# A second pair of token blocks in seven half-size products, and a weight matrix converted early and kept in DRAM

## The chip, the core and the metric

The kernel runs on one NeuronCore of a Trainium2 chip. Its engines work in parallel and each runs its own instructions in order: TensorE (PE; PEld is its weight load), VectorE (DVE), ScalarE (ACT), GpSimd (POOL) and SyncE (SP), which here issues all DMAs. The metric is the device time of one execution in microseconds (us); the compared figure is the median over runs.

## The reference

Three operators follow one another on 4 batches of 576 tokens and 512 channels (8 heads of 64), all in float32 (some weights arrive as float64).

```python
out_up    = repeat(sm_attn(mean4(q), mean4(k), mean4(v)), 4)      # pooled attention, 144 x 144
out_local = softmax(where(|i-j| < 4, q k^T / 8, -1e9)) @ v        # banded attention
x  = out_up + out_local                                           # (4, 576, 512)
u  = x + (relu(x^T @ w_tok1) @ w_tok2)^T                          # token mixing, 576 -> 256 -> 576
x  = u + relu(u @ w_ch1) @ w_ch2                                  # channel mixing, 512 -> 1536 -> 512
th = x @ w_theta
y  = w_tok_r @ (x * cos(th)) + w_tok_i @ (x * sin(th))            # per batch, 576 x 576 each
u  = x + y
result = u + relu(u @ w_ch)
```

## The kernel before, in words

**Numbers.** A float32 product is three matmuls (`mm3`, lines 142 to 146): high x high, high x low, low x high, where `high` is the value rounded to TensorE's reduced float32 and `low` the remainder. Every weight arrives as 8-byte words and goes through `converted` (line 153) one block of 128 rows at a time: a DMA into `raw`; two ScalarE steps (180, 181); three VectorE steps (183, 185, 193); one GpSimd addition (197); ScalarE's cast to `high` (199); VectorE's subtraction for `low` (201). A `yield` between these lets other work stand between them.

**Stages.** (a) Attention and token mixing, by pairs and quads of heads; the result u goes to DRAM (`uT`). (b) Channel mixing's first pass: hidden columns 0 to 511 (`LOWER` = 2 parts of 256), for six blocks of 384 tokens; the partial sum goes to DRAM (`xT`). It is interleaved with attention. (c) Channel mixing's second pass: hidden columns 512 to 1535, blocks 2 and 3, then 0 and 1, then 4 and 5. A dense block is `mix` with p0 = 2: 8 column blocks of 12 matmuls for the first layer, then 4 output blocks of 24 (lines 654 to 657). Blocks 0 and 1 are a pair: the first layer over both token blocks and halves of the channels is a 2 x 2 block product, done in seven half-size products (`pair_product`, 6 matmuls for each of 4 m). That needs sums of weight blocks (`weight_parts`, 64 steps), sums of token blocks (`pair_sum`) and additions on the way out of PSUM (`pair_hidden`). Output goes to `xT` (columns) and, transposed, to `xN` (rows). (d) The last stage, by batch: theta (lines 1081 to 1121), y (1123) with the row matrix `wr` (w_tok_r and w_tok_i, 9 blocks of 128 x 576), and the output (1183), also in seven products, with sums of `wc`.

**Order.** Stages (a) to (c) run in an order written out by hand: `ORDER` (line 30) is a list of step names, and each mention advances that step's generator to its next `yield`, so the list sets the instruction order on all five engines, SyncE's DMA issues included. Names: P, W, K, L, A: loads and steps of a head pair; V, F, T, E, U: pooled attention, token mixing, u's store; C, H, O: load, hidden and output of a block in the first pass, B, M, N in the second; S: weight sums; PL, PS, PT, PP, PH: load, split, sums, products and hidden of a pair; D: output blocks of a paired block; X: weight conversions (X8 to X23 second pass, X24 to X27 w_theta, X28 to X36 the row matrix, X37 to X40 w_ch); R: memory released and allocated; Z and ZS: batch 0 of stage (d) loaded and split. The last stage's order is set by the framework from the program's order.

In before X28 to X36 stand between D1 and N1.3 and beside B4, X24 to X27 and X37 to X40 beside B5; pools for late weights follow one another (`late_weights`, 935), and `load_x` (967) loads x and its rows xn together.

Of the kernel before, what the change touches and what calls it, by code (L numbers as in the profile page):

```python
# [41 lines left out]
X3 X6 L11*2 C0 L11 P15 U3.1*2 A8 F6 U3.1 C0 F5 T4 L11 L12 L10 O0.1 K15 C0 C1 W11 L10 O0.0 C0 T4*2 F7 O0.3 O0.2 L12 C1  # L42
O0.3 T4 L12 F7 L12 T4 C1 L11 E4.1 F6 L11 F7 L11 F6 C1 A10 W12 E4.0 L11 F6 F7 E4.0 A11 F7 L12 E4.1 C1 H1.0 T5 C2 F6
L13*2 H1.1 L12 H1.1 T4 T5 T4 U4.0 L13 C1 U4.0 H1.0 U4.0 L13 V7 T4 H1.2 T5 L13 L15 L13 T4 U4.1 L12 U4.1 L15 L12 W15 V7
C1 H1.2 A12 V7 U4.1 T5 H1.3 V7 H1.3 L13 E5.0 C1 L13 F7 C1 F7 E5.0 F7 L15 L14*2 A13 L15 C1 O1.0 L14 F7 O1.1 L14 T5 W14
C1 E5.1 C2 E5.1 T6 L14 L15 L14 T5 T6 T5 U5.0 C2 T5 U5.0 L15 U5.0 T5 O1.2 T6 O1.3*2 L15 L14 T6 U5.1 L14 U5.1*2 L15 T6
E6.0 A14 A15 C2 E6.1 C3 E6.0 T7 E6.1 T6 T7 H2.0 T6 U6.0 H2.0 T7*2 U6.0*2 C3 T6*2 T7 U6.1*2 E7.0 U6.1 C2 E7.1*2 E7.0 T7
H2.1*2 T7 U7.0 T7 U7.0*2 T7 C2*2 H2.2 U7.1 H2.2 U7.1 C3 U7.1 R0 X8 X17 H2.3 X11 H2.3 C2 X19 C2*2 X8 O2.1 X8 C2 O2.2 X8
O2.0 X11 C3 O2.3*2 X21 C3 H3.0 X19 H3.0 X19 X8 C3 X17 X8 X17 C4 H3.1 C3 H3.2*2 X17 H3.1 X19 X20 H3.3 X21 H3.3 C3 X11
X9 C3 C4 O3.0 X21 X17 X19 C3 C4 X21 C3 O3.2 X11 X21 X13 C4 O3.3 O3.1 X21 O3.3 X12 X17 X9 C4 X9 X20 X19 C4 X9 H4.0 X13  # L50
H4.0 X20 C5 C4 X15 H4.2 H4.1 X9 H4.1 X20 H4.2 H4.3 B2 X16 H4.3 C4 X9 X13 C4 C5 X13 X20 C4 O4.1 X12 X10 C5 X13 C4 O4.2
X12 B2 C5 O4.0 X12 X11 X13 C5 O4.3 H5.0 X20 X16 O4.3 X23 B2 C5 H5.1 X10 H5.0 X10 C5 H5.2 X12 X11 X10 H5.1 B2 H5.3 X14
X10 H5.3 J2 H5.2 X16 C5 M2.4 X23 X10 X16 X23 X15 C5 X18 C5 O5.1 X23 X22 B2 O5.2 O5.0 X12 X15 X14 C5 X23 X14 X16 M2.5
# [12 lines left out]
N1.0 X30 X31 N1.0*2 B4 D1 N1.1 B4 X28*2 X29 D1 N1.2 X28 X30 X29 X32 X28 X30 X29 X33 X29 N1.3 X30 X28 X29 X31 X34 N1.1
D0 N1.2 N1.1 X30 X31 D0 X32 N1.2 N0.0 X31 X30 X32 X33 X35 D0 X31 N0.1 X32 N0.0 N0.1 N0.0 X31 X32 X33 X34 X36 D0 N0.1
N0.2 X33 X32 N0.2 X35 X34 N0.2 X33 B4 N0.3 X34 X33 B4 N0.3 M4.4 X34 X35 N0.3 X36 B4 N0.3 M4.4 X35 M4.5 X34 M4.5 B4
M4.6 X36 X35 B4 M4.7 M4.6 X36 M4.7 J4 X35 X36 B4 N1.3 M4.8 N1.3 X36 M4.8 B4 M4.9 N1.3 M4.9 B4 M4.10*2 B5 M4.11*2 R6
X24 X25 X26 Z B4*2 N4.0*2 B5 N4.0 B5 X24 B4 X24 X25 N4.1 X26 X24 X25 X27 X24 X26 B4 X25 X37 X25 N4.2 X26 X24 X25 X38  # L70
X26 N4.1 B5 N4.3 N4.1 X26 B5 M5.4*2 N4.2*2 B5 M5.5 X27 M5.5 B5 X27 X37 M5.6 X37 X38 X27 B5 X39 X27 M5.6 X37 M5.7 B5
X27 M5.8 X38 X40 X37 B5 M5.9 X37 X38 M5.7 M5.8 X38 B5 M5.9 X39 X38 N4.3 M5.10 M5.11 M5.10 M5.11 X39 N4.3 X40 N4.3 X39
X40 X39*2 X40 B5 X40*2 B5 J5 R2 ZS*4 B5 ZS N5.0 N5.1 N5.0 N5.1 N5.0 ZS*2 B5 N5.2 N5.1 ZS N5.2*2 N5.3*4

# [3 lines left out]
PAIRS = ((0, 1),)  # L78
LOWER, WIDE = 2, 2
MIX = 384  # L80
# [25 lines left out]
def kernel(  # L106
# [23 lines left out]
    xN_d = dram.tile([B * S, DM], F32, name="xN")  # L130

# [21 lines left out]
    def converted(stage, hi, lo, parts, sub, add, gaps=repeat(1), room=None):  # L153

        n, at, gap = math.prod(hi.shape[1:]), next(serial), iter(gaps)
# [16 lines left out]
        if len(hi.shape) == 3:  # L172
            hi, lo = (t.rearrange("p k n -> p (k n)") for t in (hi, lo))
# [31 lines left out]
        yield  # L205

# [117 lines left out]
    weight, cells = {}, {}  # L324
    lowsteps = []
# [384 lines left out]
    def pair_room(n):  # L710
        two[n]["uh"], two[n]["ul"] = (b1.tile([128, 4, MIX], F32R, tag=f"u{p}", name=f"u{p}_p{n}") for p in "hl")

    def pair_load(n):
        i, j = PAIRS[n]
        t = two[n] = {}
        t["u"] = cells["utx"].tile([128, 4, MIX], F32, tag="ut", name=f"u_p{n}")
# [5 lines left out]
        t["th"], t["tl"] = (  # L722
            [cells["T"].tile([128, 2, MIX], F32R, tag=f"t{p}{k}", name=f"t{p}{k}_p{n}") for k in range(4)] for p in "hl"
        )
        t["last"] = t["tl"][2]
        sp.dma_start(t["last"].bitcast(F32), columns(uT_d, j)[:, 0:2])
        yield

    def pair_split(n):
        t = two[n]  # L730
        pair_room(n)
# [6 lines left out]
    def pair_sum(n, k):  # L738
# [14 lines left out]
    def pair_product(n, m, i):  # L753
# [14 lines left out]
        right = {  # L768
            1: (t["uh"][:, 0:2], t["ul"][:, 0:2]),
            2: (t["uh"][:, 2:4], t["ul"][:, 2:4]),  # L770
            3: (t["qh"], t["ql"]),
        }
        for e, k in ((5, 0), (6, 1), (7, 2), (4, 3)):
            right[e] = t["th"][k], t["tl"][k]
# [578 lines left out]
```

## Time and profile before

| | us |
|---|---|
| median of 3 runs | 685.97 |
| lowest, highest | 682.52, 691.41 |
| the profiled execution | 682.84 |
| its span, first to last instruction | 680.9 |

The profile is of one execution. PE stands for TensorE's matmuls, whose ends are modelled, so a busy PE need not be PE at its peak; DVE is VectorE, ACT ScalarE, POOL GpSimd, SP SyncE. Line numbers (L144) are those of the kernel before; a helper's line covers every use of it, and the names of the operands tell them apart (`wrl<-ww,wrh`: the low part of the row matrix from the working tile and the high part).

### The profile page before, as it was taken

How to read it: one execution, taken by the hardware profiler on the slowest of the kernel's cores; microseconds unless marked ns; L12 is line 12 of the kernel's file. 1: busy time of each engine (PE TensorE's matmuls, PEld its weight loads, DVE VectorE, ACT ScalarE, POOL GpSimd, SP SyncE). 2: the span in 40 equal slices, each digit the busy share in tenths (PEclk: the TensorE clock that was granted, in tenths of full speed). 3: DMA queues.
4: the chain of work that ended last, by engine and by line, in shares of the span. 5: the costliest groups of instructions: out<-in, count | busy, mean ns of one | idle time of the engine just before them, and what ended most of it. 6: DMA issues, size and time to landing. Idle time of an engine off the chain costs nothing.

```text
span 680.9 us, 17322 instructions
## 1 busy us (share of the span) xinstructions
PE 659.3 (97%) x7344; PEld 630.2 (93%) x7344; DVE 508.5 (75%) x916; ACT 317.2 (47%) x618; POOL 91.8 (13%) x79
## 2 busy tenths in 40 slices
PE   7869999999999999999999999999999999999997
PEld 4658879999999999999999999999998998998997
DVE  5879998764543788997656996987887848857837
ACT  4566667353442564533222553544637326526311
POOL 3223332201000432300000231330000000000000
PEclk9879999999999999999999999999999999999999
DMA  8796787554334686217434668954030420140202
GB/s 284 250 282 218 253 273 256 171 183 143 106 129 158 200 280 198 74 38 186 86 101 145 215 126 270 303 147 114 1 132 0 154 72 0 62 141 1 70 1 70
DMA packets 85629, 100.36 MB, mean 147 GB/s; under 512 B 44272, under 2 KB 65904, under 8 KB 85552
## 3 DMA queue, kind: packets, MB, share of 16 engines
q1 hardware_dynamic: 85552, 99.27, 46.5%
q8 instruction: 57, 0.93, 0.6%
q14 instruction: 20, 0.16, 0.1%
HBM read 74.34 MB, written 24.90 MB: 146 GB/s over the span
## 4 chain that ended last, share of the span: by engine, by line
PE 89%; DVE 4%; DMA 4%; ACT 1%; SPq 1%; issue 0%; POOL 0%; DVEq 0%; ACTq 0%; POOLq 0%
PE c L654 6%; PE c L144 6%; PE c L657 6%; PE c L655 6%; PE c L145 6%; PE c L146 6%; PE y L144 6%; PE y L145 6%; PE y L146 6%; PE th L144 2%; PE th L146 2%; PE th L145 2%; PE t L144 2%; PE t L146 2%; PE t L145 2%; PE c_p L849 2%
## 5 line engine op out<-in xcount | busy, mean ns | idle before, releaser
L197 POOL TENSOR_TENSOR ww<-ww,raw 128x512 int32<-128x512 int32 (+2 forms) x43 | 60.4, 1407 | 285.1 <-ACT ww L180 93.6
L144 PE MATMUL y<-wrh,zh 128*128 128x288 f32 x256 | 75.0, 296 | 0.0
L145 PE MATMUL y<-wrl,zh 128*128 128x288 f32 x256 | 74.9, 296 | 0.0
L146 PE MATMUL y<-wrh,zl 128*128 128x288 f32 x256 | 72.8, 295 | 0.0
L144 PEld LDWEIGHTS y<-wrh,zh 128*128 128x128 f32 x256 | 48.0, 188 | 0.0
L145 PEld LDWEIGHTS y<-wrl,zh 128*128 128x128 f32 x256 | 48.0, 188 | 0.0
L146 PEld LDWEIGHTS y<-wrh,zl 128*128 128x128 f32 x256 | 47.2, 188 | 0.0
L180 ACT ACTIVATE ww<-raw 128x512 f32<-128x512 f32 (+2 forms) x43 | 29.2, 679 | 30.7 <-DMA raw<-w_ch 9.8
L144 PE MATMUL c<-uh,c1h 128*128 128x384 f32 x128 | 42.8, 334 | 0.0
L146 PE MATMUL c<-uh,c1l 128*128 128x384 f32 x128 | 42.8, 334 | 0.0
L145 PE MATMUL c<-ul,c1h 128*128 128x384 f32 x128 | 42.8, 334 | 0.0
L865 DVE SCALAR_TENSOR_TENSOR g<-c,g 128x384 fp32r<-128x384 f32 x56 | 29.5, 548 | 16.8 <-ACT g L862 16.8
L862 ACT ACTIVATE g<-c 128x384 fp32r<-128x384 f32 x56 | 26.5, 490 | 28.6 <-PE c L146 28.5
L1133 DVE TENSOR_TENSOR cx<-y,cx 128x288 f32<-128x288 f32 x32 | 14.6, 456 | 32.0 <-PE y L146 31.6
L873 DVE TENSOR_TENSOR ut<-c,ut 128x384 f32<-128x384 f32 x40 | 21.4, 550 | 18.6 <-PE c L657 18.2
L139 ACT CAST cuh<-cx 128x288 fp32r<-128x288 f32 (+1 forms) x16 | 8.8, 553 | 50.3 <-DVE cx L1133 50.3
L181 ACT ACTIVATE raw<-raw 128x512 int32<-128x512 uint32 (+3 forms) x48 | 31.7, 661 | 0.0
L144 PE MATMUL th<-thh,cxh 128*128 128x512 f32 (+1 forms) x92 | 31.6, 343 | 0.0
L145 PE MATMUL th<-thl,cxh 128*128 128x512 f32 (+1 forms) x92 | 31.6, 343 | 0.0
L193 DVE SCALAR_TENSOR_TENSOR ww<-raw,ww 128x512 uint32<-128x512 uint32 (+2 forms) x43 | 30.4, 707 | 1.5
L146 PE MATMUL th<-thh,cxl 128*128 128x512 f32 (+1 forms) x92 | 31.2, 343 | 0.0
L185 DVE TENSOR_SCALAR ww<-ww 128x512 uint32<-128x512 uint32 (+2 forms) x43 | 25.0, 581 | 1.5
(361 smaller groups left out, 2110.4 us busy)
## 6 DMA issues: line engine op xcount, KB each, us to landing
raw<-w_ch SPq DMA_DIRECT2D x28, 512.0 KB
qk<-qkT SPq DMA_DIRECT2D x16, 582.0 KB
xT<-ut SPq DMA_DIRECT2D x12, 768.0 KB
vd<-vtok SPq DMA_DIRECT2D x8, 650.0 KB
raw<-w_ri SPq DMA_DIRECT2D x9, 576.0 KB
vw<-vloc SPq DMA_DIRECT2D x32, 146.2 KB
uT<-us SPq DMA_DIRECT2D x16, 288.0 KB
ut<-uT SPq DMA_DIRECT2D x6, 768.0 KB
```

The costliest lines, as they stand in the source:

```text
L144: pe.matmul(out, lh, rh, start=start, stop=False, skip_group_check=again)
L145: pe.matmul(out, lh, rl, start=False, stop=False, skip_group_check=again)
L146: pe.matmul(out, ll, rh, start=False, stop=stop, skip_group_check=again)
L180: act.activation(w, high, AF.Abs)
L181: act.activation(f, words[:, :, 0], AF.Copy, scale=2.0**-29)
L193: dve.scalar_tensor_tensor(out=wu, in0=words[:, :, 1], scalar=0xC0000000, in1=wu, op0=ALU.bitwise_and, op1=ALU.bitwise_or)
L197: pool.tensor_tensor(out=w.bitcast(I32), in0=w.bitcast(I32), in1=f, op=ALU.add)
L654: pe.matmul(ps[:, 0:MIX], h[:, cb % 2, d], h1, start=cb == cbs[0], stop=False)
L655: pe.matmul(ps[:, 0:MIX], l[:, cb % 2, d], h1, start=False, stop=False)
L657: pe.matmul(ps[:, 0:MIX], weight[cb // 2][2][:, cb % 2, d], h2, start=False, stop=cb == cbs[-1])
L862: act.activation(h1, ps, AF.Relu)
L865: dve.scalar_tensor_tensor(out=h2, in0=ps, scalar=0.0, in1=h1.bitcast(F32), op0=ALU.max, op1=ALU.subtract)
```

## The change

`PAIRS` becomes ((0, 1), (5, 4)): blocks 5 and 4 go through the pair's path instead of the dense one. The tiles of `pair_sum` are joined to one per sum; the second pair's raw u is loaded into the tile of its low part. The row matrix is converted in attention, in eleven steps X28 to X38 (nine of 512 columns, one of 8 x 64, one of 64) whose high and low parts stand in `raw` itself and are stored to DRAM (`wr_d`); they are read back by ten loads (LR) beside D4 and D5. The four blocks of w_theta are converted beside the first pair and D1, into rooms of other tiles; w_ch's first two blocks (X41, X42) likewise, kept in DRAM (`wc_d`) and read back at the end (LC), its other two (X43, X44) beside D4 and D5. Batch 0's x is loaded beside D4, its rows xn at the end of D5, when the buffer `utx` of block 4's output is free. In the last stage the split of the next x is placed after the first additions and casts of y, and the weight sums use another tile.

The order, from the first X28 on, and from D1 on (steps up to X28 stand as before, and between the two excerpts the second pass's blocks 2 and 3 and the first pair are only shuffled, with X24, X25 and X27 begun beside the pair):

```diff
-X3 X6 L11*2 C0 L11 P15 U3.1*2 A8 F6 U3.1 C0 F5 T4 L11 L12 L10 O0.1 K15 C0 C1 W11 L10 O0.0 C0 T4*2 F7 O0.3 O0.2 L12 C1
+X3 X6 X28 X29 X30 L11*2 C0 X28 L11 P15 X29 U3.1*2 A8 X28 F6 U3.1 C0 F5 T4 X29 X28 L11 L12 L10 O0.1 K15 C0 C1 X28 X29
+W11 L10 X28 X29 O0.0 C0 T4 X30 X28 T4 F7 O0.3 O0.2 L12 C1 O0.3 X31 T4 L12 F7 L12 T4 C1 L11 E4.1 F6 L11 X29 F7 L11 F6
...
+PH0.3.2 X41 X25 PL1 PH0.2.4 PL1 PH0.3.4 PL1 PH0.2.4 X25 PH0.3.4 D1*2 PH0.2.4 X25 N1.0 PH0.3.4 X25 N1.0 X27 N1.0 X25
+X27 X41 D1 X26 N1.1 X27 X41 PS1 X27 N1.1 D1 X41 N1.2 N1.1 PT1.0 X41 N1.2 X27 N1.2 X41 X26 N1.3 X41 PT1.0 X26 PT1.0 X26
+D0 N1.3 PT1.1 X26 N1.3 D0 X26 PT1.1 J0 PT1.1 N1.3 PT1.3 PS1 PT1.3 D0 PT1.3 PS1 N0.0 N0.1 N0.0 PT1.2 D0 N0.0 N0.2 PT1.2
+PS1 N0.1 PT1.2 N0.1 PP1.0.1 N0.3 N0.2 PP1.1.1 PH1.0.1 N0.2 PP1.0.3 PH1.1.1 PP1.1.3 N0.3*2 PP1.0.2 PP1.1.2 PH1.0.2 N0.3
...
+PH1.3.4 PH1.2.4 PH1.3.4 PH1.2.4 D4 PH1.3.4 R5 Z D4 N4.0 X43 LR N4.0 LR N4.0 LR D4 N4.1 LR N4.1*2 LR D4 N4.2 LR X43*2
+N4.3 R6 X43 ZS N4.2 ZS N4.2 X43 ZS X43 D5 LR ZS N4.3 LR ZS D5 X44 N5.0 N4.3 ZS N5.0 ZS N4.3 ZS LR*2 D5 N5.1*2 D5 N5.2
+X44 N5.2 X44 R6 Z X44 N5.3*2 LC X44 N5.3 X44 N5.3 LC N5.0 N5.1 N5.2
```

The code, cut to its core:

```diff
-PAIRS = ((0, 1),)
+PAIRS = ((0, 1), (5, 4))
...
+    wr_d = [dram.tile([128, 9, S], F32, name=f"wr_{e}") for e in "hl"]
+    wc_d = [dram.tile([128, 2, DM], F32, name=f"wc_{e}") for e in "hl"]
...
-    def converted(stage, hi, lo, parts, sub, add, gaps=repeat(1), room=None):
+    def converted(stage, hi, lo, parts, sub, add, gaps=repeat(1), room=None, keep=()):
...
+        if keep:
+            hi, lo = (raw.bitcast(F32R)[:, e * n : e * n + n] for e in range(2))
...
+        for dst, t in zip(keep, (hi, lo)):
+            t = t.bitcast(F32)
+            sp.dma_start(dst, t.rearrange("p (k n) -> p k n", k=dst.shape[1]) if len(dst.shape) == 3 else t)
+        if keep:
+            yield
...
+    late = []
+    for k in range(9):
+        r, c = slice(k * 128, k * 128 + 128), slice(0, 512)
+        late.append((w_ri[r, c], [t[:, k, c] for t in wr_d]))
+    c = slice(512, S)
+    late.append((w_ri[0:1024, c].rearrange("(k p) n -> p k n", p=128), [t[:, 0:8, c] for t in wr_d]))
+    late.append((w_ri[1024:1152, c], [t[:, 8, c] for t in wr_d]))
+
+    def early(k):
+        src, keep = late[k]
+        return converted(stg, None, None, [(0, 128, src)], *ENDS, keep=keep)
...
+        rooms = [(b2, "ut")] * 3 + [(cells["T"], f"t{k}") for k in (0, 1)] + [(b2, "ut")]
+        late_weights(24, range(4), rooms, w_theta, into=cells["th"])
+        late_weights(41, range(2), rooms[4:], w_ch, keep=wc_d)
...
+    def load_weights(name, d, groups):
+        for a, b in groups:
+            for t, src in zip(cells[name], d):
+                sp.dma_start(t[:, a:b].bitcast(F32), src[:, a:b])
+                yield
...
     def after_pair():
+        for name, old in (("cs", "hx"), ("cn", "utx")):
+            cells[old].release()
+            cells[name] = ctx.enter_context(tc.tile_pool(name=name, bufs=1, side="right"))
+            yield
...
     def first_load():
-        cells["x0"] = load_x(0)
+        cells["x0"] = [load_x(0)]
+        yield
+        cells["x0"].append(load_rows(0))
         yield
...
+    step("LR", lazily(lambda: load_weights("wr", wr_d, ((8, 9), (0, 2), (4, 6), (2, 4), (6, 8)))))
+    step("LC", lazily(lambda: load_weights("wc", wc_d, ((0, 2),))))
...
-    sb1 = ctx.enter_context(tc.tile_pool(name="c1p", bufs=1))
+    sb1 = ctx.enter_context(tc.tile_pool(name="c1p", reuse_waits="tile", bufs=1))
...
-            xx = load_x(b + 1)
+            x1 = load_x(b + 1)
+            with tc.issue_after(cells["x loads"].ins):
+                xx = x1, load_rows(b + 1)
             xhl, steps = split_x(b + 1, xx[0])
-            for st in steps:
-                st()
+            with tc.issue_after(added.ins), tc.issue_after(cast.ins):
+                for st in steps:
+                    st()
```

## Rows read from the trace of the kernel before

**Rows 1.** The page: busy us, share, instructions; granted clock in 40 slices.

```profile
PE 659.3 (97%) x7344; PEld 630.2 (93%) x7344; DVE 508.5 (75%) x916; ACT 317.2 (47%) x618; POOL 91.8 (13%) x79
...
PEclk9879999999999999999999999999999999999999
```

**Rows 2.** Stretches: us, PE, PEld, DVE, ACT, POOL, PEclk, DMA share, GB/s.

```profile
0.00:104.00 104.00, 86.51 (x2462) 70.50 (x2463) 87.50 (x170) 61.84 (x146) 32.15 (x35) 0.93 0.81 261
60.00:104.00 44.00, 40.65 (x1142) 35.79 (x1142) 41.11 (x79) 29.28 (x69) 13.17 (x11) 1.00 0.80 262
104.00:677.00 573.00, 572.81 (x4884) 559.72 (x4882) 419.90 (x745) 255.31 (x473) 59.61 (x44) 1.00 0.41 127
104.00:128.00 24.00, 24.00 (x471) 21.87 (x471) 21.31 (x39) 15.52 (x38) 8.76 (x8) 1.00 0.65 210
104.00:212.00 108.00, 108.00 (x1947) 102.00 (x1946) 63.59 (x115) 50.45 (x113) 12.05 (x11) 1.00 0.48 155
284.00:332.00 48.00, 48.00 (x277) 47.74 (x276) 42.87 (x89) 18.62 (x37) 1.52 (x1) 1.00 0.39 103
332.00:362.00 30.00, 30.00 (x174) 30.00 (x173) 15.59 (x30) 6.72 (x14) 0.00 (x0) 1.00 0.29 74
402.00:452.00 50.00, 50.00 (x290) 50.00 (x289) 42.20 (x65) 25.22 (x46) 12.45 (x9) 1.00 0.75 225
```

**Rows 3.** Waits of TensorE, whole span: us in total, times, longest.

```profile
PE o L523 <- DVE pbuf L501: 4.0, 1, 4.0
```

**Rows 4.** The chain in order of time: start us, us, what.

```profile
418.94 1.04 PE c L657 x6
423.10 1.04 PE c L657 x6
```

**Rows 5.** Groups of first-layer matmuls: shapes, count, busy us, mean ns.

```profile
L144 PE MATMUL c<-uh,c1h 128*128 128x384 f32 x128 | 42.8, 334 | 0.0
...
L144 PE MATMUL p_a<-uh_p,c1h 128*128 128x384 f32 x16 | 5.4, 335 | 0.0
```

**Rows 6.** Pair and eviction work of VectorE: count, ns min/median/max.

```profile
L748 DVE TENSOR_TENSOR tl_p<-z_p,th_p x4: 946/952/958, 320.3 to 331.6; 128x768 fp32r<-128x768 f32 x4
...
L735 DVE TENSOR_TENSOR ul_p<-u_p,uh_p x1: 1750/1750/1750, 325.3 to 325.3; 128x1536 fp32r<-128x1536 f32 x1
...
L873 DVE TENSOR_TENSOR ut<-c,ut x40: 512/550/560, 132.9 to 466.8; 128x384 f32<-128x384 f32 x40
```

**Rows 7.** Groups of one weight conversion's steps: busy us, mean ns | idle before.

```profile
L185 DVE TENSOR_SCALAR ww<-ww 128x512 uint32<-128x512 uint32 x32 | 17.7, 554 | 1.1
L193 DVE SCALAR_TENSOR_TENSOR ww<-raw,ww 128x512 uint32<-128x512 uint32 x32 | 22.2, 693 | 1.1
L201 DVE TENSOR_TENSOR wrl<-ww,wrh 128x576 fp32r<-128x576 f32 x9 | 13.2, 1474 | 0.0
L201 DVE TENSOR_TENSOR c11l<-ww,c11h 128x512 fp32r<-128x512 f32 x2 | 1.4, 682 | 0.0
L180 ACT ACTIVATE ww<-raw 128x512 f32<-128x512 f32 x32 | 21.6, 676 | 21.9 <-DMA raw<-w_ch 9.8 <-DVE c1l L201 9.5 <-issue 1.6
L199 ACT CAST c1h<-ww 128x512 fp32r<-128x512 f32 x8 | 4.9, 614 | 2.5 <-POOL ww L197 2.5
L197 POOL TENSOR_TENSOR ww<-ww,raw 128x576 int32<-128x576 int32 x9 | 13.0, 1442 | 114.7 <-ACT ww L180 93.6 <-DVE ww L193 9.8 <-ACT g L862 5.9
```

**Rows 8.** The timeline at the hand-over to the last stage, by engine.

```profile
466.62 0.28 PE L144 MATMUL th<-thh,cxh 128*128 128x256 f32 x1
...
471.73 0.42 DVE L1117 TENSOR_TENSOR tt<-tg,cxn 64x256 f32<-64x256 f32 x1 [2.31 <-ACT tg L1104]
...
481.72 0.68 DVE L140 TENSOR_TENSOR zl<-tf,zh 128x512 fp32r<-128x512 f32 x1
...
481.01 0.29 PE L144 MATMUL y<-wrh,eh 128*128 128x288 f32 x1
...
471.04 0.48 SPq L890 DMA_DIRECT2D xT<-ut  x1
```

More of the change, by code (lines that the diff above doesn't have):

```diff
@@ L708, with pair_room, pair_sums @@
     two = {}
-    def pair_room(n):
-        two[n]["uh"], two[n]["ul"] = (b1.tile([128, 4, MIX], F32R, tag=f"u{p}", name=f"u{p}_p{n}") for p in "hl")
+    def pair_room(n, p):
+        two[n]["u" + p] = b1.tile([128, 4, MIX], F32R, tag=f"u{p}", name=f"u{p}_p{n}")
+    def pair_sums(n, k):
+        two[n]["t", k] = t = cells["T"].tile([128, 2, 2, MIX], F32R, tag=f"t{k}", name=f"t{k}_p{n}")
+        return t
     def pair_load(n):
@@ L715, in pair_load @@
         t = two[n] = {}
-        t["u"] = cells["utx"].tile([128, 4, MIX], F32, tag="ut", name=f"u_p{n}")
+        if n:
+            pair_room(n, "l")
+            t["u"] = t["ul"].bitcast(F32)
+        else:
+            t["u"] = cells["utx"].tile([128, 4, MIX], F32, tag="ut", name=f"u_p{n}")
         sp.dma_start(t["u"], columns(uT_d, i))
@@ L721, in pair_load @@
         yield
[L722 to L725, printed above, removed]
+        t["last"] = pair_sums(n, 2)[:, 1]
         sp.dma_start(t["last"].bitcast(F32), columns(uT_d, j)[:, 0:2])
@@ L730, in pair_split @@
         t = two[n]
-        pair_room(n)
+        pair_room(n, "h")
+        if not n:
+            pair_room(n, "l")
         for p, raw in (("u", t["u"]), ("q", t["ql"].bitcast(F32))):
@@ L767, in pair_product @@
             lh, ll = x[:, a, :, c], y[:, a, :, c]
[L768 to L774, printed above, removed]
+        if i in (1, 2):
+            rh, rl = (t["u" + p][:, 2 * (i - 1) : 2 * i] for p in "hl")
+        elif i == 3:
+            rh, rl = t["qh"], t["ql"]
+        else:
+            both = t["t", (5, 6, 7, 4).index(i)]
+            rh, rl = both[:, 0], both[:, 1]
         first = i in (1, 6, 5, 3)
@@ L777, in pair_product @@
             t[m, key] = psum(m, f"p_{n}_{m}_{key}")[:, 0:MIX]
-        rh, rl = right[i]
         for kb in range(2):
@@ L853, in mix_rest @@
     def mix_rest(i):
-        ut = (cells["utx"] if i == PAIRS[0][1] else b2).tile([128, 4, MIX], F32, tag="ut", name=f"ut_{i}_{LOWER}")
+        ut = (cells["utx"] if i in [q for _, q in PAIRS] else b2).tile([128, 4, MIX], F32, tag="ut", name=f"ut_{i}_{LOWER}")
         sp.dma_start(ut, columns(xT_d, i))
@@ L1020 @@
         step(f"X{i}", st())
-    for i in range(4 * LOWER, 41):
+    for k in range(len(late)):
+        step(f"X{28 + k}", early(k))
+    for i in chain(range(4 * LOWER, 28), range(41, 45)):
         step(f"X{i}", lazily(lambda i=i: cells["X", i]()))
@@ L1068, in bank @@
         return psum(next(turns), name)
-    cells["cx"].append(ctx.enter_context(tc.tile_pool(name="cx1", bufs=1, side="right")))
-    thh, thl, wrh, wrl, wch, wcl = (cells[name] for name in ("thh", "thl", "wrh", "wrl", "wch", "wcl"))
+    cells["cx"].append(ctx.enter_context(tc.tile_pool(name="cx1", reuse_waits="tile", bufs=1, side="right")))
+    (thh, thl), (wrh, wrl), (wch, wcl) = (cells[name] for name in ("th", "wr", "wc"))
     last = {}
@@ L1261 @@
         ul = sb1.tile([128, 4, S], F32R, tag="ul", name=f"cul_{b}")
-        added = stage_y(b, 0, x, uh, ul, *z)
+        added, cast = stage_y(b, 0, x, uh, ul, *z)
         if b == 0:
```

126 lines of the change are left out of this document (59 added, 67 removed).

## The prediction, made before the changed kernel was run

> **What bounds the kernel now.** I read the busy line first [rows 1]: TensorE is busy 97% of the span, VectorE 75%, ScalarE 47%, GpSimd 13%. A busy share of TensorE is only modelled, so I went on to the stretches [rows 2] and to what TensorE waited for [rows 3]. There are two regimes. From 0 to 104 us TensorE is busy for 86.51 of 104; its longest wait, 4.0 us, is for the softmax on VectorE, and the granted clock averages 0.93. From 104 to 677 us it is busy for 572.81 of 573, at clock 1.00, with no wait in the list. Its pace there confirms that this is work and not modelled ends: two like pieces of two neighbouring groups of 24 matmuls begin at 418.94 and 423.10 [rows 4], so 24 matmuls of 384 columns take 4.16 us, 173.3 ns each, in the middle of the stretch where VectorE has its heaviest conversions. So behind 104 us time is TensorE's instruction count, and relief of another engine there is worth nothing. What can cost time is a new wait.
>
> **Part 1: seven products for blocks 5 and 4.** The dense first layer of a block in the second pass is 8 x 12 = 96 matmuls; the group of 128 per line over blocks 2 to 5, three lines, is 384 = 4 x 96 [rows 5]. A pair takes 4 x 7 x 6 = 168; the existing pair's group "a" has its 16 per line and the same 334 ns [rows 5]. Two dense blocks are 192, a pair 168: 24 fewer. The second layer stays at 24 matmuls for each of four output blocks. **Gain: 24 x 173.3 ns = 4.16 us**, all on the bounding engine. The weight sums exist already for the first pair, so none is added.
>
> What it adds is VectorE work: four sums and their remainders, at 0.95 us each, 7.6 us, the splits 1.75 + 0.95 us [rows 6], and additions in the hidden stage. The first pair's products, from 337 us on, carried theirs without a TensorE wait (the stretch 332 to 362 us [rows 2]). For the second pair I add up VectorE from D1's first output block to PP1.0.1, using the order in the diff: sums 7.6, splits 2.7 (the second, of half the size, counted at 0.95), 13 evictions and transposes of blocks 1 and 0 at 0.55, 7.2 [rows 6], two late hidden halves of the same size 1.1, and conversions: the last subtraction of w_theta's second block and three whole conversions after it, 3 x (0.55 + 0.55 + 0.69) + 4 x 0.68 = 8.1 [rows 7] (the first of the three operations has the second's form and is counted like it). That is 26.7 us against 8 output blocks x 4.16 = 33.3 us of TensorE. With GpSimd's interference added for four conversions at up to 1.44 us each it is 32.5: still covered, by 0.8 us at worst. I take 0.
>
> **Part 2: the row matrix converted in attention.** Eleven conversions enter the order between about 104 and 212 us: nine of 512 columns, one of 8 x 64, one of 64; about 10.2 full ones. Per full one ScalarE takes 0.68 twice and 0.61, 1.97 us, GpSimd 1.44, VectorE 0.55 + 0.55 + 0.69 plus 0.68 to 1.47 for the last subtraction [rows 7], so 2.5 to 3.3. Together: ScalarE 20, GpSimd 15, VectorE 25 to 33 us (10.2 times each). The stretch now holds 50.45, 12.05 and 63.59 of 108 [rows 2]; it becomes 71, 27 and 89 to 97. VectorE would be 82 to 90% busy. From 284 to 332 us it was 89% busy (42.87 of 48) and TensorE lost nothing; from 60 to 104 us it was 93% busy (41.11 of 44) and TensorE was idle 3.35 of 44, 7.6% [rows 2]. Those are the two bounds: 0 and 7.6% of 108 = 8.2 us. I take 0, because the computed share is nearest to the first row's, and TensorE's filler (the first pass of channel mixing) is already interleaved in this stretch. A gain is excluded: TensorE has no wait there to give back.
>
> DMA: nine loads of 128 x 576 x 8 bytes, 5.3 MB, move here, and as many bytes are written. 155 GB/s x 108 us = 16.7 MB becomes 27.3 MB, 253 GB/s. From 402 to 452 us 225 GB/s ran without a TensorE wait, from 60 to 104 us 262 GB/s ran beside the 3.35 us of idle [rows 2], so the same bounds apply. SyncE's queue issues 11 loads and 22 stores more; a store waits for the last subtraction, and behind it stand the loads of q, k and v, the pooled outputs' round trip through DRAM and the stores of u. At 0.48 us each, the issue of a store of u [rows 8], that is 16 us of 108: no cost while the stores' producers are on time; what it costs when they are late is inside the 8.2 us.
>
> On the last subtraction the trace shows 1474 ns for the row matrix where GpSimd ran beside it, 682 ns where the same 512-wide instruction ran alone [rows 7]. The Trainium skill (SBUF — State Buffer, "Who interferes with whom") says that a VectorE instruction with two SBUF inputs and a reading GpSimd instruction exclude each other for the whole instruction. The trace agrees in size. By that rule taken at its worst, every added GpSimd instruction would block VectorE for its whole 1.44 us, and the stretch would come to about 104 us of 108; this is the skill's argument for the first rival.
>
> **Part 3: relief later.** Nine 576-wide conversions leave the stretch behind the first pair and the theta and channel conversions spread out. TensorE had no wait there (402 to 452 us: 50.00 of 50 [rows 2]), so this is worth 0. Reading the converted row matrix back is 5.3 MB in ten DMAs beside D4 and D5 (33.3 us of TensorE); at the 225 GB/s of 402 to 452 us [rows 2] it takes 24 us. I take 0.
>
> **Part 4: the hand-over to the last stage.** In before the first theta matmul starts at 466.62, the first use of the rows xn at 471.73, y at 481.01 [rows 8], and xn was loaded long before. Now its load waits until block 4's last store has left the shared buffer. The like step of block 5 in before stored 4.4 us after its last matmul group (466.62 to 471.04) [rows 8]. Block 4's last group ends 16.6 us (D5's four output blocks) before theta starts, so its store goes out about 12 us before; 0.79 MB and then 1.31 MB of rows at 225 GB/s [rows 2] take 3.5 and 5.8 us. xn is then there about 3 us before theta starts and 8 us before its first use, less what the row matrix's last two loads ahead of it take (1.18 MB, 5.2 us). Lower bound 0. Upper bound: a load that is 5 us later than this slack, less the 1.3 us by which the last z remainder (ends 482.40) leads its use by y (21 matmuls of 288 columns after 481.01, about 483.7) [rows 8], so 3.7. I take 0. Reordered splits and tile-wise reuse in the last stage touch engines off the path: 0.
>
> **Sum.** The profiled execution took 682.84 us (span 680.9 and 1.9 around it). 682.84 - 4.16 = 678.7. The median of the three runs is 685.97, 3.13 above it, and I find nothing in the change that touches the first 104 us, where idle time and lowered clock can vary; so the forecast for a median is 685.97 - 4.16 = **681.8 us**. That is 0.6%. About 2% either way is what a measurement of this kernel can tell from no change.
>
> **The rivals.**
> - *Attention becomes VectorE-bound* (ends slower). In-order VectorE meets conversions ahead of softmax steps, and the chain of pair, pooled output and token mix arrives late at TensorE. Price at the row's worst 8.2 us: 681.8 + 8.2 = 690.0. It decides once TensorE waits over 4.16 us between 104 and 212 us. For it: the queue is already 89% busy from 104 to 128 us (21.31 of 24) [rows 2] and the skill's exclusion. Against: in that very window TensorE is busy 24.00 of 24. Chance 0.15.
> - *Late rows*: xn or the row matrix arrives late at the hand-over, 3.7 us: 685.5. It decides if xn lands over 6.4 us after theta's first matmul. For: the slack counted above is 3 us once the row matrix's last loads stand ahead. Against: each of its terms was taken in full, and the loads can overlap. Chance 0.12.
> - *The saving is not realised*: the second pair's sums come late, as the worst-case 32.5 of 33.3 us allows with one more delayed step of about 4 us, and the wait eats the 24 matmuls: 686. Chance 0.07.
> - The forecast: 0.62. The rest, 0.04, is for cases not named.
>
> **Range and chances.** Three runs of before spread from 682.52 to 691.41, -3.5 and +5.4 about their median; the forecast's own range is then 678 to 687. The first rival's full price closes the top at 690; at the bottom a little below the fastest run less the gain, 677.5. Faster by over 2% (below 672.2) would need 13.8 us and no step gives it: 0.03. Slower by over 2% (above 699.7) needs more than twice the worst row in attention: 0.05. Within 2%: 0.92.
>
> **What would show it.** TensorE's count falls from 7344 to 7320; the lines 144 to 146 of "c<-uh,c1h" fall from 128 to 64 each, the p groups double. From 104 us to the last matmul TensorE takes 4.2 us less with no wait over 0.5 us. VectorE in attention rises to 89 to 97 us; TensorE stays at full pace beside it. Behind the first pair VectorE is freer and that buys nothing. The first use of xn comes about 5 us after theta's first matmul. Wrong would be: TensorE waits of several us between 104 and 212 us, a wait of SyncE for block 4's store that ends after theta began, or a span that falls by clearly more than 4.2 us behind 104 us, which would mean that TensorE's pace was not its own.

## The result, and the profile after

The changed kernel takes **690.94 us** (median of 20 runs, 685.18 to 694.66) against 685.22 us of the kernel before on the same chips: ratio **1.0076, 95% interval 1.0054 to 1.0097**. It is 0.8% slower; 681.8 us, 0.6% faster, was forecast, and the range ended at 690.0. Ratios here and below are estimated over the single runs and need not equal the quotient of two medians (1.0083 here). The profiled execution took 693.72 us, 2.8 above the median. One execution of all the experiments, of 699.87 us in the kernel without stores, ran in a slower state and is left out of its ratio.

The page of the changed kernel, the lines that answer to [rows 1]:

```profile
PE 661.6 (96%) x7320; PEld 631.4 (91%) x7320; DVE 518.1 (75%) x952; ACT 321.5 (46%) x632; POOL 92.4 (13%) x81
...
PEclk9869999999999999999999999999999999999999
```

The 24 matmuls are gone (7344 to 7320), and yet TensorE is busy 2.3 us longer and the span 11 us longer. The stretches (columns as in [rows 2]) say where:

```profile
0.00:104.00 104.00, 86.45 (x2453) 70.39 (x2454) 86.59 (x164) 60.74 (x142) 32.59 (x35) 0.92 0.80 256
104.00:128.00 24.00, 24.00 (x419) 22.13 (x418) 21.93 (x45) 16.50 (x41) 8.54 (x8) 1.00 0.68 221
128.00:225.00 97.00, 88.68 (x1532) 83.42 (x1531) 66.87 (x120) 51.46 (x107) 16.72 (x15) 0.96 0.70 231
225.00:477.00 252.00, 252.00 (x1447) 252.00 (x1446) 187.66 (x336) 98.60 (x177) 33.28 (x23) 1.00 0.55 167
```

Time is lost only between 128 and 225 us: TensorE idles 8.3 us there, and the granted clock falls to 0.96, where before it was busy throughout at 1.00 [rows 2]. VectorE is far from full (66.87 of 97). Counted by matmuls, the 2400th and the 4500th start 127.4 us apart in the trace before and 140.5 us in this one, 13.1 us more. From the 4500th matmul to the first of y it is 252.7 before and 248.6 after: 4.1 us less, the forecast's gain, whole.

What TensorE waits for from 104 to 225 us (columns as in [rows 3]):

```profile
PE c L153 <- ACT us L636: 3.9, 1, 3.9
PE o L551 <- ACT pts L469: 2.1, 1, 2.1
PE o L551 <- issue: 1.4, 1, 1.4
```

Both named producers are short ScalarE copies (`us`: a piece of u on its way to its store; `pts`: transposed attention scores), which ran as soon as ScalarE came to them. What ScalarE itself stood for in that stretch, and SyncE's longest in total (`ut`: the columns of u of a token block, read back):

```profile
ACT ww L191 <- DMA raw<-w_ri: 11.0, 2, 6.1
ACT uh L662 <- DMA ut<-uT: 7.4, 2, 6.0
ACT us L636 <- DMA uT<-us: 6.0, 2, 3.3
...
SPq L179 <- DMA wr_l<-raw: 23.0, 7, 6.8
```

The last line says that SyncE stood 23.0 us, in seven pieces, until the stores of a `raw` buffer had landed and its next load could be asked for.

The first place, from the timeline (start, duration, engine, line, operation, tiles; idle before it in brackets):

```profile
127.88 1.39 SPq L179 DMA_DIRECT2D raw<-w_ri  x3
...
132.87 0.67 ACT L191 ACTIVATE ww<-raw 128x512 f32<-128x512 f32 x1 [4.90 <-DMA raw<-w_ri]
...
136.30 0.51 ACT L469 COPY pts<-pdt 128x384 f32<-128x384 f32 x1
...
136.86 1.12 PE L551 MATMUL o<-vw,plt 38*32 38x65 f32 x80 [2.11 <-ACT pts L469]
...
139.53 0.52 PE L683 MATMUL c<-g,c21l 128*128 128x384 f32 x1
139.84 0.52 PE L682 MATMUL c<-g,c21h 128*128 128x384 f32 x1
```

The first three raw blocks are issued at 127.88. ScalarE takes its instructions in order, reaches the conversion of the first block at 127.97, just behind the issue, and stands 4.90 us until it lands. The copies of the score transposes (pts) stand behind it, and TensorE waits for those. Then a second bill comes: the matmuls of 384 columns start every 0.32 us (139.53 to 139.84) in place of every 0.173 us [rows 4]. The second place is alike:

```profile
202.46 0.38 SPq L179 DMA_DIRECT2D raw<-w_ri  x1
203.01 0.74 SPq L655 DMA_DIRECT2D ut<-uT  x1
...
210.87 1.47 ACT L662 CAST uh<-ut 128x1536 fp32r<-128x1536 f32 x1 [5.97 <-DMA ut<-uT]
...
213.76 0.52 PE L153 MATMUL c<-uh,c10h 128*128 128x384 f32 x1 [3.88 <-ACT us L636]
```

Here SyncE's queue stood first, some 2 us, for a buffer whose store had not landed, so the columns of block 3 were asked for late, and they came 7.8 us after the issue (in the trace before at most 4.6 us, 191.44 to 196.06). ScalarE stood 5.97 us for them, with the copy `us` behind. The granted clock in the two places:

```profile
137.00:139.00 2.00, 2.00 (x86) 1.91 (x85) 2.00 (x3) 1.90 (x3) 1.20 (x1) 0.97 0.90 335
139.00:142.00 3.00, 3.00 (x11) 3.00 (x10) 2.90 (x7) 0.62 (x1) 0.12 (x1) 0.50 0.79 219
...
214.00:217.50 3.50, 3.50 (x12) 3.48 (x12) 2.43 (x7) 2.14 (x7) 1.55 (x2) 0.51 0.60 229
```

The lower of the two levels (1.2 GHz, 0.5 of 2.4) holds for some 3 us after each stand, which costs another 1.5 to 1.7 us each time. The two stands and the two slow spells together make some 9 of the 13.1 us. Of the rest, 1.4 us is the stand for which the profile names no releaser (174 us).

The groups that answer to [rows 5], and the hand-over [rows 8]:

```profile
L153 PE MATMUL c<-uh,c1h 128*128 128x384 f32 x64 | 21.4, 334 | 0.0
L153 PE MATMUL p_a<-uh_p,c1h 128*128 128x384 f32 x32 | 10.7, 335 | 0.0
```

```profile
471.50 1.34 SPq L925 DMA_DIRECT2D xT<-ut  x1
...
477.03 0.28 PE L153 MATMUL th<-thh,cxh 128*128 128x256 f32 x1
...
477.54 0.37 SPq L1017 DMA_DIRECT2D cxn<-xN  x1
...
484.62 0.41 DVE L1162 TENSOR_TENSOR tt<-tg,cxn 64x256 f32<-64x256 f32 x1
...
491.43 0.29 PE L153 MATMUL y<-wrh,eh 128*128 128x288 f32 x1
...
SPq L1017 <- DMA xT<-ut: 2.3, 1, 2.3
PE y L153 <- ACT zh L147: 0.4, 1, 0.4
```

The rows xn are used 7.6 us after theta's first matmul (5.1 before), and TensorE's only wait behind attention is 0.4 us, for the first z (last line). The load of xn was issued at 477.54, after theta had begun, because SyncE stood 2.3 us for block 4's store, itself issued only at 471.50. The way from theta to y is 14.4 us in both.

### The profile page after: what moved, and what is told of

Same layout as the page of the kernel before. It is cut to its first block, busy times and chain, and to the rows that moved or that the text cites. A ratio compares the mean times of both kernels' runs of the same rounds, so it can differ in the third digit from the quotient of the medians.

```text
span 691.9 us, 17405 instructions
## 1 busy us (share of the span) xinstructions
PE 661.6 (96%) x7320; PEld 631.4 (91%) x7320; DVE 518.1 (75%) x952; ACT 321.5 (46%) x632; POOL 92.4 (13%) x81
## 4 chain that ended last, share of the span: by engine, by line
PE 72%; DMA 12%; DVE 5%; issue 3%; ACT 3%; SPq 2%; POOL 1%; DVEq 0%; POOLq 0%; ACTq 0%
PE y L153 6%; PE y L155 5%; PE y L154 5%; PE c L154 4%; PE c L153 4%; PE c L155 4%; PE c L682 4%; PE c L683 4%; PE c L685 4%; DMA wrl<-wr_l 3%; DMA xT<-ut 2%; PE th L154 2%; PE th L153 2%; PE th L155 2%; PE c_p L884 2%
## 5 line engine op out<-in xcount | busy, mean ns | idle before, releaser
L208 POOL TENSOR_TENSOR ww<-ww,raw 128x512 int32<-128x512 int32 (+2 forms) x37 | 50.1, 1358 | 160.9 <-DVE ww L204 97.2
L208 POOL TENSOR_TENSOR raw<-raw 128x512 int32<-128x512 int32 (+2 forms) x13 | 16.6, 1273 | 184.4 <-DVE raw L204 178.1
L191 ACT ACTIVATE ww<-raw 128x512 f32<-128x512 f32 (+2 forms) x37 | 24.2, 655 | 35.8 <-DMA raw<-w_ri 11.0
L1178 DVE TENSOR_TENSOR cx<-y,cx 128x288 f32<-128x288 f32 x32 | 14.4, 455 | 30.4 <-PE y L155 29.9
L900 DVE SCALAR_TENSOR_TENSOR g<-c,g 128x384 fp32r<-128x384 f32 x40 | 21.2, 549 | 14.2 <-ACT g L897 14.2
L897 ACT ACTIVATE g<-c 128x384 fp32r<-128x384 f32 x40 | 19.2, 492 | 24.1 <-PE c L155 24.1
L194 DVE TENSOR_SCALAR ww<-ww 128x512 f32<-128x512 f32 (+2 forms) x37 | 17.1, 463 | 17.5 <-ACT ww L191 17.4
L204 DVE SCALAR_TENSOR_TENSOR ww<-raw,ww 128x512 uint32<-128x512 uint32 (+2 forms) x37 | 25.5, 690 | 1.3
L908 DVE TENSOR_TENSOR ut<-c,ut 128x384 f32<-128x384 f32 x32 | 17.1, 550 | 11.0 <-PE c L685 10.9
L551 PE MATMUL o<-vw,plt 38*32 38x65 f32 x1280 | 18.3, 233 | 6.6 <-DVE pbuf L529 2.4
L551 PEld LDWEIGHTS o<-vw,plt 38*32 38x32 f32 x1280 | 15.2, 109 | 9.9 <-DVE pbuf L529 2.8
```

Of the source, the lines that this page charges most:

```text
L191: act.activation(w, high, AF.Abs)
L204: dve.scalar_tensor_tensor(out=wu, in0=words[:, :, 1], scalar=0xC0000000, in1=wu, op0=ALU.bitwise_and, op1=ALU.bitwise_or)
L208: pool.tensor_tensor(out=w.bitcast(I32), in0=w.bitcast(I32), in1=f, op=ALU.add)
L551: pe.matmul(o[r : r + 32, 5 * j + i // 2], pts[h : h + W, i // 2, r : r + 32], vw[h : h + W, g, :], start=True, stop=True,)
L900: dve.scalar_tensor_tensor(out=h2, in0=ps, scalar=0.0, in1=h1.bitcast(F32), op0=ALU.max, op1=ALU.subtract)
```

## The experiments

Fourteen kernels. Ratios are to the kernel before, timed on the same chip, with 95% intervals. My theory at the start: ScalarE and SyncE, served in order, stand before landings, at two places, and could be reordered. Rival: the sum of the added engine work, VectorE's above all. A third: the transfers themselves. The "lag" of the expectations is how much later the n-th matmul starts than in the trace of the kernel before, both counted from the 2400th. Ranges given in us go by 685.2 us for the kernel before, so I judge them by ratio.

**Taking parts away.** First, the pair without any of the conversions in attention.

```diff
-        step(f"X{28 + k}", early(k))
+        step(f"X{28 + k}", iter(()))
```

The row matrix read back later is then two other halves, stored behind attention so that the transfers there stay.

> The kernel after without X28 to X38: nothing of the row matrix is converted or moved in attention; the ten late loads read w_tok2's split halves (stored once to DRAM behind attention) in its place, so y is not the reference's. Theory (attention alone costs): the second pair gives its 24 matmuls, 4.2 us less than before, about 681, ratio 0.994, and TensorE has no new wait between 104 us and the end of attention. Rival A (the pair or the hand-over costs too): 685 or more.

Measured 682.08 us, **0.9933 (0.9897 to 0.9968)**. Attention is as before: 121.00 of 121 us busy.

```profile
104.00:225.00 121.00, 121.00 (x2021) 114.94 (x2020) 69.59 (x129) 54.62 (x122) 13.09 (x12) 1.00 0.52 171
```

So the pair is worth what the sum said, 4.6 us here, nothing behind attention takes it back, and the conversions cost 1.0076 - 0.9933 = 1.43%, 9.8 us. All of the following are read against 0.9933; the difference of two ratios is known to 0.4 or 0.5%. The 9.8 us can so be 7.0 to 12.6, and smaller steps in what follows are not told from nothing.

The transfers alone (11 loads, 22 stores of the unconverted words, no engine work):

```diff
+        sp.dma_start(raw..., src)
+        for _ in range(6):
+            yield
+        for e, dst in enumerate(keep):
+            sp.dma_start(dst, raw.bitcast(F32)[:, e * n : e * n + n]...)
```

> As e1, but X28 to X38 load the raw block and store its two halves unconverted at the steps where the converted ones are stored: the DMAs and SyncE's issues of after, none of its ScalarE, VectorE and GpSimd work. Theory (ScalarE, in order, stands before a conversion whose load has not landed, and SyncE before a store whose data is not ready): most of the loss goes, 682 to 685. Rival B (DMA traffic alone delays u and the pooled outputs): the loss stays, 688 to 691.

Measured 688.73 us, 1.0010 (0.9979 to 1.0042): +0.77% on the pair alone, over my theory (682 to 685 us, up to 0.9997) and under rival B (688 to 691 us, from 1.0041). ScalarE does not work on the raw blocks here, and still stands longer for attention's own transfers than in the kernel before, whose two lines stand below:

```profile
ACT uh L671 <- DMA ut<-uT: 9.8, 3, 4.6
ACT us L645 <- DMA uT<-us: 9.2, 4, 3.9
...
ACT uh L634 <- DMA ut<-uT: 2.6, 1, 2.6
ACT us L608 <- DMA uT<-us: 4.4, 2, 3.6
```

Loads and engine work, without the stores (`for dst, t in zip(keep, ...)` runs over nothing in attention):

> As after, but the converted halves of X28 to X38 are not stored; the late loads read w_tok2's halves. Loads and all engine work stay. Theory: the wait of ScalarE for a raw load at about 132 us stays (some 4 us with the clock), SyncE's blocking before the late load of u goes: 684 to 687. Rival C (VectorE's load is the cause): 689 to 691, as after. Rival B (traffic): about half the loss, 685 to 688.

Measured 690.35 us, 1.0035 (1.0005 to 1.0065): +1.02%. As a ratio that is rival B's range (685 to 688 us, 0.9997 to 1.0041), over my theory's and under rival C's.

The reverse: the kernel before, with the whole of the attention work added to its order (as Y28 to Y38), stored and never read.

> The kernel before with the conversions X28 to X38 and their stores added in attention in the places of after; nothing reads them, and the row matrix is converted late as well. Theory: it carries after's whole loss in attention and none of its gain, 685.2 + 9.9 = 695. Rival A (the loss arises behind attention): 685 to 687.

Measured 697.56 us, **1.0135 (1.0075 to 1.0195)**: 9.3 us, where 9.9 was expected. The attention work by itself carries the whole loss.

**Moving steps.** First the two places by themselves and together, in the changed kernel's written order (cut to its core; #n is here the step's number, from 0; a load is #0, ScalarE's first step #1; the first two blocks' later steps move back a little with them):

```diff
-X28#1 L11 P15 X29#1 U3.1*2 A8 X28#2 F6#4 U3.1 C0 F5 T4#0
+L11 P15 U3.1*2 A8 F6#4 U3.1 C0 F5 T4#0 X28#1 X29#1 X28#2
...
-U5.1 X34#6 X35 ... X37#0 E6.1 C3#0 ... U6.0 C3#1 ... U6.1*2
+U5.1 C3#0 X34#6 X35 ... X37#0 E6.1 ... U6.0 ... U6.1*2 C3#1
```

> The changed kernel with seven entries of the written order moved: ScalarE's first conversion steps of the first two row-matrix blocks (X28, X29) go behind the score-transpose copies F6 and the cast T4 that they stand ahead of, and their later steps with them. Nothing is added or left out. Theory (ScalarE, in order, stood 4.9 us before the landing of a raw block at 128 to 133 us, and the pts copies behind it held TensorE 2.1 us and dropped its clock): the lag against the kernel before no longer grows by 4 us between matmuls 2940 and 3400, the wait of 'o' for the pts copies of 2.1 us goes, and the time is some 4 us under the changed kernel's: 686 to 688, ratio to the kernel before 1.001. Rival (contention of the 33 added transfers, or the sum of the added engine work, whatever the order): within 1 us of the changed kernel, ratio 1.006 to 1.008.

> The changed kernel with two entries of the written order moved: the load of block 3's first-layer columns (C3) goes ahead of two stores of X34 and the raw load of X37 on SyncE's queue, and its cast on ScalarE behind the two copies of U6.1. Nothing is added or left out. Theory (the load stood behind raw loads that wait for a buffer to be stored, landed late, and ScalarE stood 6.0 us before it with the U6.1 copies behind): TensorE's wait of 3.9 us at 210 to 214 us and the half clock behind it go, the lag does not step by 5.7 us between matmuls 4320 and 4380, and the time is some 5 us under the changed kernel's: 685 to 687, ratio 1.000. Rival (contention, or the sum of the work): another wait of like size within the next 10 us, ratio 1.005 to 1.008.

> Both moves together, in the changed kernel. Theory: both steps of the lag go, some 9 us under the changed kernel's time: 680 to 683, ratio 0.990 to 0.996, that is as fast as the kernel with the second pair and no conversions in attention (0.9933). Rival (bandwidth or engine time is what is short): 687 to 690, ratio 1.001 to 1.006, with the lag at matmul 4380 still over 8 us.

Measured 1.0117 (1.0073 to 1.0161), 1.0146 (1.0097 to 1.0196) and 1.0134 (1.0090 to 1.0179). My theory of two faulty places falls: none is faster than the changed kernel, and each lies over its rival's range too. The stands moved: with the first change the wait for pts is gone, and others have come. With both changes TensorE waits for

```profile
PE c L154 <- ACT us L637: 4.8, 1, 4.8
PE sd L418 <- DVE x L566: 2.8, 1, 2.8
```

The first is the second place again, now held by another landing on ScalarE, of the raw block that SyncE could only ask for at 211.33, when its buffer's store had landed:

```profile
204.54 0.38 SPq L220 DMA_DIRECT2D wr_l<-raw  x1
211.33 0.38 SPq L180 DMA_DIRECT2D raw<-w_ri  x1
...
215.18 0.66 ACT L192 ACTIVATE ww<-raw 128x512 f32<-128x512 f32 x1 [7.31 <-DMA raw<-w_ri]
```

The second is new: VectorE stood 2.9 us for ScalarE's first conversion step and then ran six steps of two conversions, with the division of the attention outputs behind them.

The stores on ScalarE's queue in place of SyncE's (`sp.dma_start(dst, ...)` becomes `act.dma_start(dst, ...)`):

> The changed kernel with the 22 stores of the row matrix issued by ScalarE in place of SyncE, at the same places of the written order; nothing is left out. It takes 22 DMA issues (about 0.45 us each, 10 us) off SyncE's queue and puts them on ScalarE's. Theory A (SyncE's queue held up by the stores is the larger part): uT stores and ut loads go out earlier, the step at matmul 4320 to 4380 falls below 2 us, ratio 1.000 to 1.004. Theory B (ScalarE's stand before landings is the larger part): ScalarE now stands for VectorE's low halves as well, the steps stay or grow, ratio 1.007 to 1.012.

Measured 1.0093 (1.0056 to 1.0130): as theory B had it. Taking the 22 issues off SyncE gave nothing back; since ScalarE carries them here, this does not show that they cost nothing on SyncE.

All conversion steps of attention put anew, with 7 us for each landing:

> The changed kernel with the written order of all the row matrix's attention steps (X28 to X38) put anew, and nothing added or left out: each load stands about 7 us ahead of its first ScalarE step, each buffer's next load at least 7 us behind its stores (the landings that the trace of the changed kernel shows: 4.9 to 8 us), and ScalarE's and VectorE's steps lie in gaps of those engines in the trace of the kernel with the second pair alone. Theory A (the order allowed too little for landings; with three stage buffers and real landings it can still be met): the lag between matmuls 2400 and 4500 stays under 4 us (13.2 in the changed kernel), ratio 0.993 to 0.999. Theory B (transfers in flight and VectorE's added work hold the path wherever they stand; moving single steps only moved the stall): the lag there grows by 8 to 14 us, ratio 1.004 to 1.012.

Measured 692.50 us, 1.0095 (1.0067 to 1.0122): theory B's range. The waits turn up in yet other places (the list of TensorE's waits has plt, h and x). My estimate of why: a buffer is held for a landing of 7 us, some 8 us of engine steps and a store's 7 us, so three buffers allow a conversion every 7 to 8 us, and eleven take some 81 of the 85 us. No run with more buffers tests this.

**Engine work against transfers.** All engine work, three loads, no stores:

```diff
+            again = keep and "mmw" not in cells and len(raws) == 3
+            if again:
+                raw = raws[turn[0] % 3][:, 0:n]
...
+            if not (keep and again):
                 sp.dma_start(dst, src)
```

> The second pair, and in attention the engine work of all eleven conversions, but only the first three load (the other eight work again on these three buffers, at their places in the order) and none stores; the row matrix is replaced by other halves, so the values differ. So 30 of the 33 added transfers are left out. Theory (the engines have room, landings are what holds them): lag between matmuls 2400 and 4500 under 2 us, ratio 0.993 to 0.996. Rival 1 (VectorE's added 31 us and ScalarE's 22 us hold TensorE by themselves, above all at 120 to 150 us, where VectorE is busy 15 of 20 us before): lag 4 to 6 us there, ratio 0.999 to 1.004.

Measured 0.9989 (0.9957 to 1.0022): +0.56%, just under rival 1's range. To see whether that is VectorE's, the same with its four instructions under `if not (keep and "mmw" not in cells):`

> The kernel with the engine work alone (three loads, no stores), with VectorE's four instructions of each attention conversion left out too: ScalarE's three, GpSimd's one and the three loads stay; the row matrix is replaced by other halves. Engine work alone cost 0.56% against the second pair alone (0.9989 against 0.9933, 3.8 us). If that is VectorE (25 us of its time, and what stands behind it): ratio 0.993 to 0.995. If it is ScalarE's stand before the first load at 128 to 133 us and its 22 us of work: ratio 0.997 to 1.000, and the lag still steps by 2 us between matmuls 2940 and 3000.

Measured 1.0001 (0.9969 to 1.0033), +0.68%: taking all of VectorE's added work away gave nothing back that could be measured. The stand at the first three loads is there without it:

```profile
136.48 0.67 ACT L202 ACTIVATE ww<-raw 128x512 f32<-128x512 f32 x1 [5.20 <-DMA raw<-w_ri]
...
141.17 1.12 PE L564 MATMUL o<-vw,plt 38*32 38x65 f32 x80 [3.10 <-ACT pts L482]
```

And with all engine work, but those three loads replaced by a memset (`dve.memset(raw.bitcast(F32), 1.0)`):

> The kernel with the engine work alone, with its last three loads replaced too, by a VectorE memset of the same three buffers (about 1 us each): all of ScalarE's, VectorE's and GpSimd's attention work of the eleven conversions, no transfer at all; the row matrix is replaced by other halves. If ScalarE's stand before the first load's landing was the whole cost of the engine work (0.56 to 0.68% in the two kernels that kept the three loads, with and without VectorE's instructions): no step of the lag between matmuls 2940 and 3120, ratio 0.992 to 0.995, as the second pair alone (0.9933). If steps in queues served in order cost without any transfer: ratio 0.998 to 1.001.

Measured **0.9942 (0.9914 to 0.9970)**: +0.09%, nothing that can be told from the pair alone. The step from the three loads to none, 0.47%, is itself barely over what two ratios can tell. VectorE is fuller here than in any other kernel of the study, and 98% busy for 20 us:

```profile
104.00:225.00 121.00, 117.68 (x2107) 110.63 (x2107) 98.81 (x173) 72.38 (x154) 25.44 (x22) 1.00 0.50 163
...
140.00:160.00 20.00, 18.00 (x396) 16.41 (x378) 19.51 (x35) 11.59 (x26) 2.66 (x2) 1.00 0.52 159
...
PE sd L431 <- DVE x L579: 1.7, 1, 1.7
```

This one profiled execution, of 686.2 us span, was not free: TensorE idles 3.3 of the 121 us, 1.7 of it in a wait for VectorE. The twelve runs, 680.94 to 688.66, are what the 0.09% rests on.

**How many, and where.** The first five conversions at their places:

> The second pair, and in attention only the first five of the eleven conversions (X28 to X32: loads, engine work, stores, at their places in the order); X33 to X38 are left out and the row matrix is replaced by other halves. The loss of all eleven is 1.43% (9.8 us). If it is the sum of the work, five of the nine full blocks cost half, some 5 us: ratio 1.000. If it is the first stand at 128 to 133 us that costs 4 us and the rest comes from the later ones: lag 4 us by matmul 3120 and flat from there on, ratio 0.999. If the ring of three buffers is what fails, with five conversions in 85 us nothing is short: lag under 2 us, ratio 0.994 to 0.996.

Measured 1.0023 (0.9999 to 1.0047): +0.90%, most of the loss for half of the work. In the trace the lag grows by 4.0 us to matmul 3120, as the second answer had it, but by 2.9 more behind it; the ratio is over the first answer's. And six, none before 140 us, with 9 us for each landing:

> The second pair, and in attention six of the eleven conversions (five full blocks and the 64-column rest of eight), all of them placed in the stretch 140 to 200 us, where the kernel before has VectorE busy 10.5 of 20 us and the transfers at 0.32 to 0.39 of the 16 engines from 160 us on; each load 9 us ahead of its ScalarE step, each buffer free 9 us before its next load. The other five are left out and the row matrix is replaced by other halves. The first five at their old places cost 0.90% against the second pair alone (1.0023 against 0.9933). If the place and the distances are what costs: lag between matmuls 2400 and 4500 under 1.5 us, ratio 0.993 to 0.997. If each conversion costs wherever it stands (transfers that land later, steps in queues that are served in order): lag 4 to 6 us, ratio 1.000 to 1.004.

Measured 0.9989 (0.9961 to 1.0016): +0.56%, between the two. The place and the distances seem to help (0.34% for one conversion more, against an uncertainty of 0.4%), but do not make the transfers free.

One comparison runs through the traces, one of each kernel. TensorE stands for the pts copies, for 1.7 to 3.1 us, in each of the eight kernels in which ScalarE converts the first three loaded blocks at their places in the changed kernel: the changed kernel, that without stores, the kernel before with the work added, the second place moved alone, stores on ScalarE, three loads with and without VectorE, the first five. It does not in the six others that add work: with transfers but no ScalarE work on them, with ScalarE's work but no transfers, and in the four whose order has these steps elsewhere. So the first place needs both, a landing and a ScalarE step put in front of it.

The ledger, above the pair alone (each line known to 0.4 or 0.5%):

| in attention | loads | engine work | stores | above 0.9933 |
|---|---|---|---|---|
| engine work, no transfer | 0 | 11 | 0 | 0.09% |
| engine work, three loads | 3 | 11 | 0 | 0.56% |
| the same without VectorE | 3 | 11, ScalarE and GpSimd | 0 | 0.68% |
| transfers alone | 11 | 0 | 22 | 0.77% |
| no stores | 11 | 11 | 0 | 1.02% |
| the changed kernel | 11 | 11 | 22 | 1.43% |

Engine work costs nothing that the runs can tell until there are transfers to stand for: 0.09% alone, but 1.43 - 0.77 = 0.66% (0.3 to 1.0) on top of the transfers. A single trace is a poorer witness: the 2400th and the 4500th matmul start 131.4 us apart in the profiled execution without transfers and 131.7 in that of the transfers alone, 127.3 in that of the pair alone. No version that computes the reference and beats the kernel before was found; 0.9933 leaves the conversions out. Converting some blocks behind the second pair, where the row matrix is read back anyway, was not tried.

## Why the prediction was wrong

**Part 1, right.** 24 matmuls fewer, 4.16 us forecast; 4.1 us less from the 4500th matmul to y in the trace, 0.67% (4.6 us) in the runs of the pair alone. The second pair's sums stayed covered: TensorE busy 252.00 of 252 us.

**Part 2, the step that failed: "I take 0, because the computed share is nearest to the first row's".** The cost was 9.8 us (7.0 to 12.6), where it was put at 0 with an upper bound of 8.2. The busy times came out near those computed (VectorE 21.93 + 66.87 = 88.80 us between 104 and 225 us, against 89 to 97; 221 and 231 GB/s against 253), but the argument asked whether VectorE is full, and that was not the main question: at 98.81 of 121 us without transfers the runs show no loss. The transfers got one sentence by bandwidth ("the same bounds apply") and one by issues ("no cost while the stores' producers are on time"). The trace of before had the warning: the idle time of the conversion's first step there is 21.9 us, 9.8 of it for landings of raw blocks (the ScalarE row of [rows 7]). I read that row for its 676 ns and not for what stood ahead of it. That idle time was free in the kernel before: between 104 and 225 us ScalarE stood 7.7 us there, up to 6.3 at once, for raw blocks (the line below, of the kernel before), and TensorE lost nothing. The added steps stand ahead of the copies us, pts and plt, for which TensorE waits.

```profile
ACT ww L180 <- DMA raw<-w_ch: 7.7, 2, 6.3
```

**Part 3, right.** Relief behind the first pair was worth 0.

**Part 4, right in its price and wrong in its working.** Of the late rows' 3.7 us bound 0.4 us came. But the sum had block 4's store go out some 12 us before theta began and the rows there 3 us before it; the store went out 5.5 us before (471.50), and the load of xn was issued 0.5 us after theta began, which the prediction itself named as a sign of being wrong. VectorE reached the rows 7.6 us after theta began, not 5, and did not stand for them. That so much less slack cost only 0.4 us is luck as far as the working goes.

**The rivals.** *Attention becomes VectorE-bound* had the place and nearly the price (8.2, 690.0), and its point of decision was passed: TensorE's waits there come to over 4.16 us. Its mechanism is refuted as the main cause: transfers without any added VectorE work cost 0.77%, VectorE's and all other engine work without transfers 0.09%. Whether VectorE has a part in the 0.66% that engine work costs beside the transfers was not tested; waits of TensorE for VectorE of 1.7 to 2.8 us do turn up in some traces (the moved steps, the kernel without transfers). The exclusion between VectorE and GpSimd of the Trainium skill (SBUF — State Buffer, "Who interferes with whom") was the support for it; with eleven more GpSimd instructions in the stretch and no transfer, no time was lost that the runs can tell. (The prediction set 1474 ns of a 576-wide subtraction beside 682 ns of a 512-wide one and called the width the same; 576-wide ones without GpSimd took 710 and 745 ns in that trace, so the reading holds.) What was missing among the rivals is a fourth: in-order queues that stand before landings.

**What is shown and what is not.** Shown: the loss lies in attention, most of it needs the transfers, more than half of it comes without VectorE's work (by the means: 0.77 of 1.43%), and moving one or two steps does not give it back. That the first place's stand passes through ScalarE standing before a landing is shown by the kernels with and without the loads and the ScalarE steps. How the whole cost divides between standing for the new blocks, SyncE standing for its buffers' stores, and attention's own transfers landing later stays open.

## What to carry to other kernels

Cost a moved step by what it waits for, not only by its busy time: count the landings that an in-order engine is put in front of, and name what stands behind it on that engine. Engine time that is free in one stretch is not free to an instruction with a transfer ahead of it; here stands of 4.9 to 7.3 us for a landing reached TensorE as 2.1 to 4.8 us, and as much as 1.7 more came by the clock. When moving the stalled step only moves the stall, take the resource away (here the transfers) before looking for a better order.

## What the runs showed of the hardware

- After a stand of TensorE of 2.1 us (or 3.9) the granted clock was 0.50 (0.51) for some 3 us, and matmuls of 384 columns started every 0.32 us, not 0.173. After the first stand this began 2.3 us behind the restart (136.86 to 139.2), with TensorE busy in between; after the second, at the restart.
- In the stretch that ran at 231 GB/s a transfer of 0.79 MB (ut) landed 7.8 us after its issue; in the kernel before, at 155 GB/s, the same transfer took at most 4.6 us. The stores of a raw buffer (0.26 MB each) held SyncE, and the buffer's next load, for up to 6.8 us.
- The same kernel's executions spread over some 9 us (685.18 to 694.66; before, 682.52 to 691.41). Much of it can arise ahead of the change: the 2400th matmul, up to which all kernels follow the same order, starts between 99.7 and 108.1 us in the sixteen traces. One profile cannot weigh a change of a few us; the runs have to.
